# Crossbar DMAs in place of TensorE transposes for q, k and the attention output of the last five half batches of a fused attention and feed-forward kernel

## Chip, cores and metric

One core of one Trainium2 chip. The metric is device time in microseconds (us), median of several runs; lower is better. Most runs of one kernel lie within 1% of each other. Ratios are the mean time of one kernel's runs over the mean of the other's in the same rounds, so they are not quite the ratio of the medians that are quoted beside them.

In the profile PE is TensorE (PEld its weight loads), DVE VectorE, ACT ScalarE, POOL GpSimd, and SPq the queue from which SyncE issues DMAs. L709 is line 709 of the kernel's file. PSUM is the memory that PE writes its results to. A DMA lands when its data has arrived. A crossbar transpose is a DMA that transposes on the way (`dma_start_transpose`). The two kernels have different line numbers for the same statement, so each line below is told in words too.

## The reference

Sliding-window attention with four sink positions, then a gated feed-forward layer on all tokens. Batch 4, 8 heads, 768 tokens, head size 64, model width 512, hidden width 2048.

```python
scores = scale * np.matmul(q, k.transpose(0, 1, 3, 2))
keep = is_sink | in_window                       # 4 sinks, window of 128
a = softmax(np.where(keep, scores, -1e9))
attn = np.matmul(a, v)
x = attn.transpose(0, 2, 1, 3).reshape(B * S, H * D)
h = x @ w_in
return (h * (1 / (1 + np.exp(-beta * h)))) @ w_out
```

Inputs and output are float32; the kernel computes its matmuls in bfloat16.

## The kernel before

The work is cut into 8 half batches of 384 tokens, and each half batch into 4 pairs of heads (32 units `u`). For a unit: transpose q and k (`T`), scores (`SC`, `SS`), weighted values (`AV`), transpose the output (`OT`). When four units are done, a half batch can go through the feed-forward layer (`HQ`, then `OQ`). The kernel does not run in the order of the source: while it is built, a planner (`Graph`) records all operations with an estimated time each, lists them per engine in the order of a simulated run, and emits that order. On the chip each engine executes its own list in order, whatever is ready.

The q and k of a unit go through PE into a PSUM bank and are copied out by DVE or ACT; the output goes the same way:

```python
def T(u):                                       # 6 transposes and one copy of 128x768
    hb, hp = u // 4, u % 4
    bs = take(1)                                # a PSUM bank
    mp = P[:, bs[0], :].bitcast(BF16)
    for i, n in enumerate("qk"):
        for c in range(NK):
            add("pe", lambda e, i=i, n=n, c=c: nc.tensor.transpose(
                mp[:, i * HALF + c * 128:i * HALF + (c + 1) * 128],
                x16[n][hb % NX][:, c, 2 * hp:2 * hp + 2, :].rearrange("p h d -> p (h d)"), ident[:, :]),
                mm_ns(128), r=[(n + "16", hb % NX, hp, c), "ident"], x=[("B", bs[0])])
    any_of(copies(qkT[u % NT]..., mp[:, 0:2 * HALF]..., {"dve": 868, "act": 690}),
           w=[("qkT", u % NT)], x=[("B", bs[0])])
    # ... (cut)

def OT(u):                                      # 3 transposes and one copy of 128x384
    # ... (cut)
    for m in range(NK):
        add("pe", lambda e, m=m: nc.tensor.transpose(
            mp[:, m * 128:(m + 1) * 128], onorm[on][:, m, :, :].rearrange("p h d -> p (h d)"), ident[:, :]),
            mm_ns(128), r=[("on", on), "ident"], x=[("B", bs[0])])
    any_of(copies(xT[:, hp, t0:t0 + HALF], mp[:, 0:HALF], {"dve": 407, "act": 370}),
           w=[("xT", hp, 2 * b + half)], x=[("B", bs[0])])
```

All DMAs are issued from SyncE. The planner charges each of them 550 ns of that queue, and its bytes to one shared stream:

```python
def place(self, o, at):
    o.at = at
    if o.dma:
        self.free[o.eng] = at + (1150 if o.eng == "gp" else 550)
        self.dma_free = max(self.dma_free, at + 1100) + 1.15 * o.ns
        o.end = self.dma_free + 1000
    else:
        o.end = self.free[o.eng] = at + o.ns
```

The softmax here doesn't subtract the row's maximum and nothing guards it: scores larger than these inputs give would overflow.

## Time and profile before

240.95 us median (240.21 to 241.29, 4 runs); the profiled run had a span of 239.3 us.

| what | before |
|---|---|
| PE busy | 228.4 us, 95% of the span |
| PE busy from 50 to 230 us | 10.00 of every 10 us, save one stretch each of 9.96 and 9.74 |
| DVE / ACT / POOL busy | 62% / 68% / 33% |
| DMA engines | full until about 101 us, then 2 to 15% in most stretches |
| transposes on PE | 288 (192 of q and k, 96 of the output) |

The first view is the table of stretches: from and to in us, its length, then for PE, PEld, DVE, ACT and POOL the busy us with the number of instructions in brackets, the clock granted to PE, the share of the DMA engines, GB/s.

```profile
40.00:50.00 10.00, 8.80 (x51) 4.52 (x50) 8.57 (x18) 6.61 (x12) 0.66 (x1) 1.00 1.08 332
...
90.00:100.00 10.00, 10.00 (x94) 6.06 (x92) 7.44 (x16) 8.42 (x17) 1.87 (x5) 1.00 1.12 267
...
120.00:130.00 10.00, 10.00 (x113) 6.33 (x110) 6.47 (x14) 7.40 (x15) 3.58 (x9) 1.00 0.07 26
```

In the first 50 us PE still waits; from 50 us on it never stops. What PE does less of there should come off the time one for one, and what DVE and ACT do less of should not.

The cost of a transpose on this full PE is not the duration that the groups list. Groups (line, engine, operation, output and inputs, shapes, count, busy us, mean ns; then idle time before it) and the timeline of PE (start, us, what, count):

```profile
L690 PE MATMUL P<-ident,onorm 128*128 128x128 bf16 x96 | 10.7, 220 | 2.3 <-DVE onorm L677 2.2
```

```profile
113.88 0.34 PE L548 MATMUL P<-ident,q_0 128*128 128x128 bf16 x3
114.06 0.33 PE L548 MATMUL P<-ident,k_0 128*128 128x128 bf16 x3
114.22 1.03 PE L729 MATMUL P<-w_out,g 128*128 128x512 bf16 x4
```

One transpose is listed with 220 ns, but three q and three k transposes start at 113.88 and the next work starts at 114.22: 0.34 us for six, 57 ns each. They overlap in the engine. In the chain of waits 24 of them in a row account for 1.34 us, 56 ns each.

### The profile page before, as it was taken

Reading aid. Unit: us, or ns where it says so; the run is one execution under the profiler, and the core shown is the slowest. Engines: PE = TensorE matmul, PEld = TensorE weight load, DVE = VectorE, ACT = ScalarE, POOL = GpSimd, SP = SyncE. Lnnn points to the kernel's source line nnn. Section 1 sums busy time; section 2 is a strip of 40 time slices with the busy share of each in tenths; the row PEclk is TensorE's granted clock in tenths of the full one; section 3 lists DMA queues with packets and bytes.
Section 4 is the critical chain, followed back from the end, with each engine's and each line's share of the span. In section 5 each row is a group of like instructions: output and inputs, shape, how many; then the busy total and the mean of one; then the engine's idle time right before and its main releaser. Section 6 shows DMA issues by size and latency. Waiting matters only on the chain.

```text
span 239.3 us, 4895 instructions
## 1 busy us (share of the span) xinstructions
PE 228.4 (95%) x1936; PEld 132.3 (55%) x1936; DVE 149.4 (62%) x305; ACT 163.7 (68%) x293; POOL 79.6 (33%) x172
## 2 busy tenths in 40 slices
PE   7977898999999999999999999999999999999994
PEld 5554554556565666565566555565555555555541
DVE  3895598886896987898667585464433633443320
ACT  3858977679788888997768686856544644554431
POOL 6575933032875593263643043530000000000000
PEclk9999999999999999999999999999999999999999
DMA  6999999999999999801011010110111011011112
GB/s 169 255 341 230 313 394 386 337 218 337 240 286 249 315 313 285 180 4 45 4 44 45 2 44 3 44 47 0 47 44 44 18 42 40 36 44 47 44 44 88
DMA packets 49558, 33.87 MB, mean 142 GB/s; under 512 B 25968, under 2 KB 42368, under 8 KB 49536
## 3 DMA queue, kind: packets, MB, share of 16 engines
q1 hardware_dynamic: 49536, 33.57, 48.6%
q8 instruction: 15, 0.25, 0.5%
q14 instruction: 7, 0.06, 0.1%
HBM read 27.27 MB, written 6.29 MB: 140 GB/s over the span
## 4 chain that ended last, share of the span: by engine, by line
PE 80%; SPq 9%; DVE 4%; DMA 3%; ACT 2%; issue 1%
PE P L729 34%; PE P L709 31%; SPq L491 7%; PE P L600 4%; PE P L548 4%; PE P L671 3%; DMA g<-in_moe_w_in_dram 3%; PE P L690 2%; SPq L501 2%; DVE g L716 1%; PE P L632 1%; PE P L661 1%; ACT t L714 1%; ACT E L609 1%; DVE w_in L438 1%
## 5 line engine op out<-in xcount | busy, mean ns | idle before, releaser
L716 DVE SCALAR_TENSOR_TENSOR g<-t,P 128x384 bf16<-128x384 f32 x128 | 69.9, 552 | 59.2 <-ACT t L714 56.6
L714 ACT ACTIVATE t<-P,hbeta 128x384 f32<-128x384 f32 x128 | 74.0, 587 | 44.5 <-PE P L709 41.1
L709 PE MATMUL P<-xT,w_in 128*128 128x384 bf16 x512 | 98.5, 326 | 1.1 <-DVE w_in L438 1.0
L729 PE MATMUL P<-w_out,g 128*128 128x512 bf16 x384 | 97.3, 379 | 0.0
L615 POOL TENSOR_SCALAR_AFFINE_SELECT E<-E 128x512 bf16<-128x512 bf16 (+1 forms) x112 | 54.5, 516 | 56.1 <-ACT E L609 55.3
L709 PEld LDWEIGHTS P<-xT,w_in 128*128 128x128 bf16 x512 | 48.0, 98 | 37.5 <-DVE w_in L438 1.8
L729 PEld LDWEIGHTS P<-w_out,g 128*128 128x128 bf16 x384 | 36.5, 98 | 33.3 <-DVE g L716 0.5
L609 ACT ACTIVATE E<-P 128x768 bf16<-128x768 f32 x64 | 45.7, 769 | 3.1 <-PE P L600 2.8
L438 DVE COPY qkT<-P 128x768 bf16<-128x768 bf16 x19 | 18.0, 951 | 4.0 <-PE P L548 4.0
L671 PE MATMUL P<-vaug,E 128*128 128x65 bf16 x352 | 18.8, 193 | 0.8 <-DVE vaug L438 0.7
L433 ACT ACTIVATE osb<-P 128x512 f32<-128x512 f32 x21 | 12.5, 597 | 10.2 <-PE P L729 10.1
L671 PEld LDWEIGHTS P<-vaug,E 128*128 128x128 bf16 x352 | 16.7, 97 | 3.4 <-DVE vaug L438 0.9
L677 DVE TENSOR_TENSOR onorm<-P,rden 128x384 bf16<-128x384 f32 x32 | 17.8, 557 | 1.0
L600 PE MATMUL P<-qkT 64*128 64x128 bf16 (+1 forms) x256 | 16.3, 239 | 1.0 <-ACT E L609 0.9
L433 ACT ACTIVATE xT<-P 128x384 bf16<-128x384 bf16 x20 | 9.9, 495 | 6.7 <-PE P L690 6.7
L600 PEld LDWEIGHTS P<-qkT 64*128 64x128 bf16 x256 | 8.6, 94 | 10.6 <-issue 5.1
L433 ACT ACTIVATE qkT<-P 128x768 bf16<-128x768 bf16 x13 | 10.2, 814 | 5.2 <-PE P L548 5.1
L635 ACT ACTIVATE ES<-P 128x128 bf16<-128x128 f32 (+1 forms) x32 | 12.1, 407 | 2.2 <-PE P L632 2.1
L690 PE MATMUL P<-ident,onorm 128*128 128x128 bf16 x96 | 10.7, 220 | 2.3 <-DVE onorm L677 2.2
L661 PE MATMUL P<-vS,ES 128*128 128x130 bf16 x64 | 12.7, 220 | 0.0
L690 PEld LDWEIGHTS P<-ident,onorm 128*128 128x128 bf16 x96 | 7.0, 98 | 7.7 <-DVE onorm L677 4.2
L885 PE MATMUL P<-ones 128*128 128x256 bf16 x47 | 8.8, 323 | 1.1 <-POOL ones L444 1.1
(60 smaller groups left out, 148.3 us busy)
## 6 DMA issues: line engine op xcount, KB each, us to landing
v_stage<-in_v_dram SPq DMA_DIRECT2D x24, 256.0 KB, 6.7
out_dram<-osb SPq DMA_DIRECT2D x24, 256.0 KB, 2.0
q_stage<-in_q_dram SPq DMA_DIRECT2D x7, 768.0 KB, 6.8
k_stage<-in_k_dram SPq DMA_DIRECT2D x7, 768.0 KB, 8.6
wst<-in_moe_w_in_dram SPq DMA_DIRECT2D x5, 512.0 KB, 8.9
wst<-in_moe_w_out_dram SPq DMA_DIRECT2D x4, 512.0 KB, 6.8
g<-in_moe_w_out_dram SPq DMA_DIRECT2D x4, 512.0 KB, 6.9
g<-in_moe_w_in_dram SPq DMA_DIRECT2D x3, 512.0 KB, 8.2
```

The source lines that it names most:

```text
L433: return lambda e: e.activation(dst, src, AF.Copy, bias=0.0, scale=scale)
L438: return lambda e: e.tensor_copy(dst, src)
L600: add("pe", lambda e, dst=dst, kt=kt, kc=kc, rows=rows, q0=q0, nq=nq: e.matmul(dst, kt[rows, 1, kc:kc + 128], qkT[u % NT][rows, 0, q0:q0 + ...
L609: add("act", lambda e, src=src, dst_=dst_: e.activation(dst_, src, AF.Exp, bias=0.0, scale=SCALE), act_ns(256 * n), w=[(k_, z, j) for k_ i ...
L615: add("gp", lambda e, d=d, sg=sg, at_=at_: e.affine_select(d, d, [[0, 2 * len(at_)], [sg, 128]], ALU.is_ge, 0.0, base=min(sg, 0), channel_ ...
L671: e.matmul(A[:, c0:c0 + D + 1], E[z][:, i, hh, :], vaug[vz][:, kb % NK, 2 * hp + hh, :], start=a, stop=o, skip_group_check=True), 39,
L677: add("dve", lambda e: e.tensor_tensor(onorm[on][:, :, :, :].rearrange("p m h d -> p (m h) d"), av[:, :, 0:D], rden[on][:, :].unsqueeze(2) ...
L690: add("pe", lambda e, m=m: nc.tensor.transpose(mp[:, m * 128:(m + 1) * 128], onorm[on][:, m, :, :].rearrange("p h d -> p (h d)"), ident[:, ...
L709: add("pe", lambda e, c=c: e.matmul(hp, w_in16[:, c, m * 128:(m + 1) * 128], xT[:, c, t0:t0 + HALF], start=(c == 0), stop=(c == 3)), mm_ns ...
L714: add("act", lambda e: e.activation(tt[ti][:, :], hp, AF.Tanh, bias=0.0, scale=hbeta[:, m:m + 1]), act_ns(HALF) + 93, r=["hbeta"], w=[("t" ...
L716: add("dve", lambda e: e.scalar_tensor_tensor(gt[T_ % NG][:, m, :], tt[ti][:, :], 1.0, hp, ALU.add, ALU.mult), dve_ns(HALF), r=[("t", ti)] ...
L729: add("pe", lambda e, m=m: e.matmul(P[:, bk, :], gt[T_ % NG][:, m, t * 128:(t + 1) * 128], w_out16[:, m, :], start=(m == 0), stop=(m == NM ...
```

## The change

Its intent: take 180 of the 288 transposes off PE, with the copies out of PSUM that belong to them, and let the DMA engines, idle after 101 us, do them. The first three half batches stay on PE, since the DMA engines are full then. The core of the diff (cut):

```diff
-            self.free[o.eng] = at + (1150 if o.eng == "gp" else 550)
+            self.free[o.eng] = at + o.hold
 ...
+    CUT = 3
 ...
+    def XP(hb, n, c):
+        z0, i = 4 * hb % NT, "qk".index(n)
+        src = x16[n][hb % NX][:, c, :, :].rearrange("p h d -> p (h d)")      # 128 x 512
+        dst = qkT[:, z0:z0 + 4, i, c * 128:(c + 1) * 128]
+        add("sp", lambda e: e.dma_start_transpose(dst, src), 950,
+            r=[...], w=[...], dma=f"x{n}{hb % 3}{c}", hold=1310)
 ...
     def OT(u):
+        if u >= 4 * CUT:
+            dst = xT[:, hp, t0:t0 + HALF].rearrange("p (m t) -> p m t", m=NK)
+            src = onorm[on][:, :, :, :].rearrange("p m h d -> p (m h d)")     # 128 x 384
+            add("sp", lambda e: e.dma_start_transpose(dst, src), 750, r=[("on", on)],
+                w=[...], dma=f"xo{on}", hold=1310)
+            return
```

So the new DMAs are 30 of 128x512 (four 128x128 tiles; one third of q or k of a half batch) and 20 of 128x384 (three tiles; the output of one unit). The planner charges each 1.31 us of the SyncE queue (`hold`) and 1.15 x 950 or 750 ns of the DMA stream. Three things come along: q and k of the last five half batches are loaded in blocks of 128 tokens, 256 KB each with runs of 256 bytes, instead of 768 KB with runs of 768 bytes; there are 12 instead of 8 slots for transposed q and k and 5 instead of 3 for outputs; and the transposed outputs are kept for 5 half batches instead of all 8, to pay for that.

More of the change, by code (lines that the diff above doesn't have):

```diff
@@ L24 @@
     __slots__ = ("eng", "fn", "deps", "signal", "count", "waits", "sem", "vc", "dma", "seq", "end", "ns", "alts",
-                 "group", "tail", "preds", "ready", "left", "succ", "at")
+                 "group", "tail", "hold", "preds", "ready", "left", "succ", "at")
 class Graph:
@@ L52, in begin, with add @@
         self.group += 1
-    def add(self, eng, fn, ns=0, r=(), w=(), x=(), dma=None, alts=None):
+    def add(self, eng, fn, ns=0, r=(), w=(), x=(), dma=None, alts=None, after=(), hold=550):
         o = Op()
@@ L60, in add @@
         o.eng, o.fn, o.dma, o.ns, o.alts = eng, fn, dma, ns, alts or {eng: (fn, ns)}
-        o.signal, o.count, o.waits, o.vc = False, 0, [], None
+        o.signal, o.count, o.waits, o.vc, o.hold = False, 0, [], None, hold
         o.group = self.group if eng == "pe" else None
@@ L71, in add @@
             deps += [(p, False) for p in self.writers.get(k, ())]
+        for k in after:
+            deps += [(p, False) for p in self.readers.get(k, []) + self.writers.get(k, [])]
         for k in x:
@@ L346, in _program @@
     NU = 2 * NPAIR
-    NSTG, NX, NV, NT, NE, NON, NG, NTT, NOS, NKS, NWS = 2, 2, 3, 8, 4, 3, 3, 3, 4, 4, 6
+    NSTG, NX, NV, NT, NE, NON, NG, NTT, NOS, NKS, NWS = 2, 2, 3, 12, 4, 5, 3, 3, 4, 4, 6
+    NXT = 5
+    CUT = 3
     FAST = 1
@@ L357, in _program @@
     headm = sb("headm", (128, 2), BF16)
-    xT = sb("xT", (128, 4, NTOK), BF16)
+    xT = sb("xT", (128, 4, NXT * HALF), BF16)
     w_in16 = sb("w_in16", (128, 4, DF), BF16)
     w_out16 = sb("w_out16", (128, NM, NOUT), BF16)
-    stg = {n: sb(n + "_stage", (128, H, NK, D), F32, NSTG) for n in "qk"}
-    stg["v"] = sb("v_stage", (128, NK, H, D), F32, NSTG)
+    stg = {n: sb(n + "_stage", (128, NK, H, D), F32, NSTG) for n in "qkv"}
+    stg_p = {n: [t[:, :, :, :].rearrange("p a b d -> p (a b d)").rearrange("p (h j d) -> p h j d", j=NK, d=D)
+                 for t in stg[n]] for n in "qk"}
     x16 = {n: sb(n + "16_", (128, NK, H, D), BF16, NX) for n in "qk"}
     vaug = sb("vaug", (128, NK, H, D + 1), BF16, NV)
-    qkT = sb("qkT", (128, 2, HALF), BF16, NT)
+    qkT = sb("qkT", (128, NT, 2, HALF), BF16)
     E = sb("E", (128, 6, 2, 128), BF16, NE)
@@ L380, in _program, with add @@
     P = ps("P", (128, 8, 512))
-    def add(eng, fn, ns, r=(), w=(), x=(), dma=None):
-        return G.add(eng, fn, ns, r, w, x, dma)
+    def add(eng, fn, ns, r=(), w=(), x=(), dma=None, after=(), hold=550):
+        return G.add(eng, fn, ns, r, w, x, dma, None, after, hold)
     def any_of(alts, r=(), w=(), x=()):
@@ L482, in load @@
         b, t0, z = hb // 2, hb % 2 * HALF, hb % NSTG
-        if n == "v":
-            src = v[b, :, t0 + i * 128:t0 + (i + 1) * 128, :].rearrange("h p d -> p h d")
-            dst, keys, ns = stg[n][z][:, i, :, :], [i], 262144 / 240
+        if n == "v" or hb >= CUT:
+            src = {"q": q, "k": k, "v": v}[n][b, :, t0 + i * 128:t0 + (i + 1) * 128, :].rearrange("h p d -> p h d")
+            dst, keys, ns = stg[n][z][:, i, :, :], [("stb", n, z, i)], 262144 / 240
         else:
@@ L488, in load @@
             src = {"q": q, "k": k}[n][b, hs, t0:t0 + HALF, :].rearrange("h (p j) d -> p h (j d)", j=NK)
-            dst = stg[n][z][:, hs, :, :].rearrange("p h j d -> p h (j d)")
+            dst = stg_p[n][z][:, hs, :, :].rearrange("p h j d -> p h (j d)")
             keys, ns = ([i], 196608 / 350) if i is not None else (range(4), 786432 / 350)
-        add("sp", lambda e: e.dma_start(dst, src), ns,
-            w=[("stg", n, z, j) for j in keys], dma=f"d{n}{z}{'' if i is None else i}")
+            keys = [("stg", n, z, j) for j in keys]
+        after = [("stg", n, z, j) for j in range(4)] if hb in range(CUT, CUT + NSTG) and n != "v" else ()
+        add("sp", lambda e: e.dma_start(dst, src), ns, w=keys, dma=f"d{n}{z}{'' if i is None else i}", after=after)
     def load_w(j):
@@ L516, in cast @@
             src, dst = stg[n][z][:, i, :, :], vaug[hb % NV][:, i, :, 0:D]
-            r, w = [("stg", n, z, i), ("vones", hb % NV)], [("v", hb % NV, i)]
+            r, w = [("stb", n, z, i), ("vones", hb % NV)], [("v", hb % NV, i)]
         elif hb == 0:
             hs = slice(2 * i, 2 * i + 2)
-            src = stg[n][z][:, hs, :, :].rearrange("p h j d -> p j h d")
+            src = stg_p[n][z][:, hs, :, :].rearrange("p h j d -> p j h d")
             dst = x16[n][hb % NX][:, :, hs, :]
@@ L523, in cast @@
         else:
-            src, dst = stg[n][z][:, :, i, :], x16[n][hb % NX][:, i, :, :]
-            r, w = [("stg", n, z, j) for j in range(4)], [(n + "16", hb % NX, j, i) for j in range(4)]
-        if hb == 0 and n != "v":
-            ns = {"act": 413, "dve": 400}
-        else:
-            ns = {"act": 540, "dve": 340, "gp": 612}
+            dst, w = x16[n][hb % NX][:, i, :, :], [(n + "16", hb % NX, j, i) for j in range(4)]
+            if hb >= CUT:
+                src, r = stg[n][z][:, i, :, :], [("stb", n, z, i)]
+            else:
+                src, r = stg_p[n][z][:, :, i, :], [("stg", n, z, j) for j in range(4)]
+        ns = {"act": 413, "dve": 400} if hb == 0 and n != "v" else {"act": 540, "dve": 340, "gp": 612}
         any_of(copies(dst, src, ns), r=r, w=w)
@@ L537, in cast, with qk_keys, first_keys @@
                     r=[("vS", z), ("v", hb % NV, 0)], w=[("vSd", z, hh)])
+    def qk_keys(u, name="qkT", every=NT):
+        return [(name, u % every, a, c) for a in range(2) for c in range(NK)]
+    def first_keys(u):
+        ks = u % NKS
+        kd = kS[ks][:, :].rearrange("p (a w) -> p a w", w=32)[:, 0:2, 0:NSINK]
+        add("gp", lambda e: e.tensor_tensor(
+            kd, qkT[:, u % NT, 1:2, 0:NSINK].to_broadcast([128, 2, NSINK]),
+            headm[:, :].unsqueeze(2).to_broadcast([128, 2, NSINK]), ALU.mult), 200,
+            r=[("kS", ks), ("qkT", u % NT, 1, 0), "headm0", "headm"], w=[("kSd", ks)])
+    def XP(hb, n, c):
[3 more added lines that the diff above has]
+        add("sp", lambda e: e.dma_start_transpose(dst, src), 950,
+            r=[(n + "16", hb % NX, j, c) for j in range(4)], w=[("qkT", z0 + j, i, c) for j in range(4)],
+            dma=f"x{n}{hb % 3}{c}", hold=1310)
+        for j in range(4):
+            mark(("qkTu", 4 * hb + j, i, c), ("qkT", z0 + j, i, c))
+        if hb % 2 == 0 and (n, c) == ("k", 0):
+            for j in range(4):
+                first_keys(4 * hb + j)
     def T(u):
@@ L551, in T @@
                     mm_ns(128), r=[(n + "16", hb % NX, hp, c), "ident"], x=[("B", bs[0])])
-        any_of(copies(qkT[u % NT][:, :, :].rearrange("p a (s j) -> p a s j", j=NK),
+        any_of(copies(qkT[:, u % NT, :, :].rearrange("p a (s j) -> p a s j", j=NK),
                       mp[:, 0:2 * HALF].rearrange("p (a j s) -> p a s j", a=2, j=NK), {"dve": 868, "act": 690}),
-               w=[("qkT", u % NT)], x=[("B", bs[0])])
+               w=qk_keys(u), x=[("B", bs[0])])
+        for key in qk_keys(u):
+            mark(("qkTu", u) + key[2:], key)
         if hb % 2 == 0:
-            ks = u % NKS
-            kd = kS[ks][:, :].rearrange("p (a w) -> p a w", w=32)[:, 0:2, 0:NSINK]
-            add("gp", lambda e: e.tensor_tensor(
-                kd, qkT[u % NT][:, 1:2, 0:NSINK].to_broadcast([128, 2, NSINK]),
-                headm[:, :].unsqueeze(2).to_broadcast([128, 2, NSINK]), ALU.mult), 200,
-                r=[("kS", ks), ("qkT", u % NT), "headm0", "headm"], w=[("kSd", ks)])
+            first_keys(u)
         give(bs)
@@ L591, in SC @@
                 own = u if kb >= NK * half else u - 4
-                kt = qkT[own % NT]
+                kt = qkT[:, own % NT, 1, :]
                 kc = (kb % NK) * 128
@@ L600, in SC @@
                     add("pe", lambda e, dst=dst, kt=kt, kc=kc, rows=rows, q0=q0, nq=nq: e.matmul(
-                        dst, kt[rows, 1, kc:kc + 128],
-                        qkT[u % NT][rows, 0, q0:q0 + 128 * nq].rearrange("p (s w) -> p s w", w=128),
+                        dst, kt[rows, kc:kc + 128],
+                        qkT[rows, u % NT, 0, q0:q0 + 128 * nq].rearrange("p (s w) -> p s w", w=128),
                         start=True, stop=True), mm_ns(128 * nq) / 2 + 24,
-                        r=[("qkT", u % NT), ("qkT", own % NT)], x=[("B", bs[2 * j + hh])])
+                        r=qk_keys(u) + (qk_keys(own) if own != u else []), x=[("B", bs[2 * j + hh])])
         for j, grp in enumerate(GROUPS[half]):
@@ L631, in SS @@
         bs = take(1)
-        add("pe", lambda e: e.matmul(P[:, bs[0], q0:HALF], kS[ks][:, :], qkT[u % NT][:, 0, q0:HALF], start=True,
+        add("pe", lambda e: e.matmul(P[:, bs[0], q0:HALF], kS[ks][:, :], qkT[:, u % NT, 0, q0:HALF], start=True,
                                      stop=True), mm_ns(HALF - q0),
-            r=[("kSd", ks), ("qkT", u % NT)], x=[("B", bs[0])])
+            r=[("kSd", ks)] + qk_keys(u), x=[("B", bs[0])])
         add("act", lambda e: e.activation(ES[z][:, q0:HALF], P[:, bs[0], q0:HALF], AF.Exp, bias=0.0, scale=SCALE),
@@ L686, in OT @@
         on = u % NON
+        t0 = (2 * b + half) % NXT * HALF
+        if u >= 4 * CUT:
+            dst = xT[:, hp, t0:t0 + HALF].rearrange("p (m t) -> p m t", m=NK)
+            src = onorm[on][:, :, :, :].rearrange("p m h d -> p (m h d)")
+            add("sp", lambda e: e.dma_start_transpose(dst, src), 750, r=[("on", on)],
+                w=[("xT", hp, (2 * b + half) % NXT)], dma=f"xo{on}", hold=1310)
+            return
         bs = take(1)
@@ L692, in OT @@
                 mm_ns(128), r=[("on", on), "ident"], x=[("B", bs[0])])
-        t0 = b * S + half * HALF
         any_of(copies(xT[:, hp, t0:t0 + HALF], mp[:, 0:HALF], {"dve": 407, "act": 370}),
-               w=[("xT", hp, 2 * b + half)], x=[("B", bs[0])])
+               w=[("xT", hp, (2 * b + half) % NXT)], x=[("B", bs[0])])
         give(bs)
@@ L705, in HQ @@
         bs = take(1)
-        t0 = T_ * HALF
+        t0 = T_ % NXT * HALF
         hp = P[:, bs[0], 0:HALF]
@@ L711, in HQ @@
                 start=(c == 0), stop=(c == 3)), mm_ns(HALF),
-                r=[("w16", m // 4, c // 2), ("xT", c, T_)], x=[("B", bs[0])])
+                r=[("w16", m // 4, c // 2), ("xT", c, T_ % NXT)], x=[("B", bs[0])])
         spare_ = [("wst", NWS // 2 + z) for z in range(NWS // 2)] if (T_, m) == (NG - 1, 0) else []
@@ L746, in xl @@
         if hb:
+            if hb >= CUT:
+                return [(hb, n, c) for n in "qkv" for c in range(NK)]
             return [(hb, "q", None), (hb, "k", None)] + [(hb, "v", c) for c in range(NK)]
@@ L753, in _program @@
     OS = [(T_, t, j) for T_ in range(NSB) for t in range(3) for j in range(4)]
-    n_cast, n_w = [0], [0]
+    XPS = [(hb, n, c) for hb in range(CUT, NSB) for n in "qk" for c in range(NK)]
+    n_cast, n_w, n_x = [0], [0], [0]
     BACKLOG, AHEAD, MARGIN = 6000, 300, 200
@@ L760, in head @@
         if s == "T":
-            if i >= NU or i - NT + 4 >= min(done["SC"], done["SS"]):
+            if i >= 4 * CUT or i - NT + 4 >= min(done["SC"], done["SS"]):
                 return None
@@ L766, in head @@
             tb = banks_at(1)
-            fn = lambda: (T(i), mark(("qkTu", i), ("qkT", i % NT)))
+            fn = lambda: T(i)
         elif s in ("SC", "SS"):
@@ L770, in head @@
                 return None
-            t, tb = G.at([("qkTu", i)]), banks_at(4 if s == "SC" else 1)
+            t, tb = G.at(qk_keys(i, "qkTu", NU) + ([("kSd", i % NKS)] if s == "SS" else [])), banks_at(4 if s == "SC" else 1)
             fn = lambda: (SC if s == "SC" else SS)(i)
@@ L781, in head @@
             t, tb = G.at([("onu", i)]), banks_at(1)
-            fn = lambda: OT(i)
+            if t and i >= 4 * CUT:
+                t, tb = 0, 0
+            if i // 4 >= NXT and done["H"] < NM * (i // 4 - NXT + 1):
+                return None
+            fn = lambda: (OT(i), mark(("xTu", i % 4, i // 4), ("xT", i % 4, i // 4 % NXT)))
         elif s == "H":
@@ L788, in head @@
                 return None
-            t = G.at([("xT", c, T_) for c in range(4)] + [("w16", m // 4, 0), ("w16", m // 4, 1)])
+            t = G.at([("xTu", c, T_) for c in range(4)] + [("w16", m // 4, 0), ("w16", m // 4, 1)])
             tb = banks_at(1)
@@ L825, in background @@
                     load(*x)
-                    mark(("in",) + x, ("stg", x[1], x[0] % NSTG, x[2] or 0))
+                    mark(("in",) + x, ("stb" if x[1] == "v" or x[0] >= CUT else "stg", x[1], x[0] % NSTG, x[2] or 0))
                     done["load"] += 1
@@ L831, in background @@
                 hb, n, c = CASTS[i]
-                t = G.at([("in", hb, n, None if n != "v" and hb else c)])
+                t = G.at([("in", hb, n, None if n != "v" and 0 < hb < CUT else c)])
                 ok = done["T"] >= 4 * (hb - NX + 1) if n != "v" else done["AV"] >= 4 * (hb - NV + 2)
@@ L837, in background @@
                     moved = True
+            if n_x[0] < len(XPS):
+                hb, n, c = XPS[n_x[0]]
+                if n_cast[0] > CASTS.index(XPS[n_x[0]]) and min(done["SC"], done["SS"]) >= 4 * (hb - NT // 4 + 2):
+                    XP(hb, n, c)
+                    n_x[0] += 1
+                    moved = True
+                    if n_x[0] % 6 == 0:
+                        done["T"] += 4
             if n_w[0] < 16:
@@ L847, in _program @@
         load(*x)
-        mark(("in",) + x, ("stg", x[1], 0, x[2]))
+        mark(("in",) + x, ("stb" if x[1] == "v" else "stg", x[1], 0, x[2]))
         if n_ == 1:
@@ L854, in _program @@
     done["load"] = 11
-    def T_(u):
-        T(u)
-        mark(("qkTu", u), ("qkT", u % NT))
     for u in range(2):
@@ L863, in _program @@
         cast(0, "k", u)
-    T_(0)
-    T_(1)
+    T(0)
+    T(1)
     beta_in()
@@ L871, in _program @@
         SS(u)
-        T_(u + 2)
+        T(u + 2)
     SC(2)
@@ L884, in _program @@
     OT(3)
+    for c in range(4):
+        mark(("xTu", c, 0), ("xT", c, 0))
     G.fill(lambda e: e.matmul(P[:, 7, 0:256].rearrange("p (a b) -> p a b", a=2), ones[:, :],
```

## The prediction

> **What bounds the kernel now.** TensorE (PE). In the table of stretches PE is busy 10.00 of 10 us in nearly every stretch from 50 to 230 us, at a granted clock of 1.00; only the first 50 us (7.5 to 9.8 of 10) have idle time. The chain of waits agrees: 80% PE. DVE (62%), ACT (68%) and POOL (33%) are off the path after 50 us. The DMA engines are full until about 101 us and nearly idle afterwards.
>
> **What the change removes.** For half batches 3 to 7 (20 of 32 head pairs) it removes 6 q/k transposes and 3 output transposes each: 180 of 288 on PE. A matmul's listed time (220 ns) includes pipeline latency; the cost on a full PE is the spacing. In the chain 24 of them take 1.34 us, 56 ns each; in the timeline six take 0.34 to 0.35 us. So 180 x 56 ns = 10.1 us, all after about 60 us, where PE is the limit. Also gone are 20 PSUM evictions of qkT (0.95 us on DVE, 0.81 on ACT) and 20 of xT (0.35 or 0.50): about 27 us off DVE and ACT, which gives slack, no time.
>
> **What it adds.** 30 crossbar transposes of 128x512 and 20 of 128x384 bf16, 5.9 MB, on the SyncE queue; the planner charges each 1.31 us of queue and about 1 us of DMA: 65 us of a queue that today mostly waits for output evictions (133 us). q and k of those half batches are loaded in 256 KB blocks of 256-byte runs, like v, instead of 768 KB of 768-byte runs. Where only v was in flight (94 to 100 us) the DMA moved 225 to 256 GB/s; with q and k 330 to 370. So a half batch's loads cost an estimated 9.6 us instead of 7.5. With transposes (10 us) and output that is 20 to 23 us of DMA per half batch: the DMA stays busy until about 170 us, but the PE has some 24 us of work per half batch, and its order holds feed-forward matmuls between a transpose and its reader.
>
> **Critical path.** All 10.1 us come out, less about 1 us of new stalls (the PE order is fixed). The first 50 us stay. Prediction: 240.98 - 10.1 + 1 = 231.9 us; range 229.5 to 237. Faster by over 2%: 0.81; within 2%: 0.14; slower: 0.05.
>
> **What would show it.** PE busy near 218; 108 transposes left; PE still 10.00 of 10 from 50 us on; DMA share high to 165-175 us; q/k transposes issued in about 1.3 us each, landed 4 to 6 us later; DVE and ACT together 27 us less busy; no PE wait above 1 us on qkT or xT.
>
> **What would make it wrong.** The cost of a crossbar transpose; no trace here shows one. The Trainium skill, "VectorE: DVE Perf Modes", section "The three transpose paths", gives 1309 ns for one 128x128; 180 tiles one after the other at that price (estimate from that page) would need 236 us. The skill's "DMA: Bandwidth & Descriptors", section "Latency and other measured facts", gives 261 GB/s; then 5.9 MB need 23 us (estimate from that page). I take the planner's middle value. If transposes take 1.5 times as long, or hold up loads behind them, lateness adds up over five half batches and PE waits at the scores (readers of qkT) between 70 and 180 us: 233 to 242 us. Another risk: output stores blocking the in-order queue.

## The result

232.51 us median (231.59 to 234.15, 4 runs) against 240.95; ratio 0.9661, 95% interval 0.9602 to 0.972. Repeated on the set of runs of e5 below: 232.44 us (231.33 to 232.95, 6 runs), ratio 0.9629, interval 0.9596 to 0.9663. The prediction was 231.9 us, in a range of 229.5 to 237.

| what | before | after |
|---|---|---|
| time, median | 240.95 us | 232.51 us |
| span of the profiled run | 239.3 us | 230.6 us |
| PE busy | 228.4 us | 216.6 us |
| DVE / ACT / POOL busy | 149.4 / 163.7 / 79.6 us | 135.0 / 156.6 / 73.3 us |
| transposes on PE | 288 | 108 |
| DMA packets | 49,558 | 94,997 |

PE's records lack 26 of the 384 matmuls of the second feed-forward matrix (1730 records beside 1756 weight loads). Each lost record leaves a hole of about 0.05 us, which is why the stretches read 9.95 and not 10.00 even where nothing waits. The table of stretches after:

```profile
40.00:50.00 10.00, 8.86 (x49) 4.44 (x50) 8.56 (x17) 6.66 (x11) 0.66 (x1) 1.00 1.08 333
...
90.00:100.00 10.00, 9.56 (x72) 5.15 (x70) 6.67 (x16) 6.67 (x15) 1.36 (x2) 1.00 0.83 198
...
120.00:130.00 10.00, 9.09 (x55) 4.71 (x55) 5.10 (x12) 7.04 (x15) 0.66 (x1) 1.00 1.14 238
```

The start is the same. Two stretches lose time to waits, 90 to 100 and 120 to 130; the DMA engines, which before were at 7 or 8% from 110 to 170 us, now stay busy until about 180 us.

The issues of the transposes and how long they hold the queue, from the answers for the tiles of transposed q and k and of the outputs (duration in ns, minimum, median and maximum; then from issue to landing):

```profile
L564 SPq DMA_TRANSPOSE qkT<-q x15: 1258/1267/2106, 58.7 to 164.6; - x15
L564 SPq DMA_TRANSPOSE qkT<-k x15: 1264/1267/2151, 62.2 to 165.9; - x15
...
DMA to landing us min/median/max: 2.5/2.6/4.5
```

```profile
L721 SPq DMA_TRANSPOSE xT<-onorm x20: 1179/1253/1907, 91.6 to 189.6; - x20
...
DMA to landing us min/median/max: 2.3/2.7/4.7
```

The planner's 1.31 us of queue was right (1.27 us and a gap of some 0.05 us). It lands after 2.6 us, and PE does not wait for a transpose's landing: the list of PE's waits has no DMA in it. What it does have is this:

```profile
PE P L727 <- DVE onorm L707: 2.0, 3, 1.0
PE P L765 <- DVE g L752: 1.3, 2, 0.9
PE P L581 <- DVE k L444: 1.1, 2, 0.8
PE P L935 <- POOL ones L450: 1.1, 1, 1.1
```

(Columns: who waited, for whom, us in total, times, longest.) The first and the last two waits lie in the first 50 us; from 50 to 80 us PE waits for nothing. The second is new: two waits, 1.3 us together, of the second feed-forward matmul for `g`, the activation that DVE writes. The longer of the two is at 124.5 us. DVE's timeline there:

```profile
118.47 2.50 DVE L752 SCALAR_TENSOR_TENSOR g<-t,P 128x384 bf16<-128x384 f32 x4 [0.96 <-ACT t L750]
123.27 0.43 DVE L444 CAST vaug<-v_stage 128x512 bf16<-128x512 f32 x1 [2.29 <-DMA v_stage<-in_v_dram]
124.45 0.43 DVE L444 CAST vaug<-v_stage 128x512 bf16<-128x512 f32 x1 [0.74 <-DMA v_stage<-in_v_dram]
124.79 1.94 DVE L752 SCALAR_TENSOR_TENSOR g<-t,P 128x384 bf16<-128x384 f32 x4
```

and the SyncE queue before that:

```profile
112.95 6.26 SPq L721 DMA_TRANSPOSE xT<-onorm  x4
119.25 0.58 SPq L774 DMA_DIRECT2D out_dram<-osb  x1
119.87 2.13 SPq L499 DMA_DIRECT2D v_stage<-in_v_dram  x3
```

Four transposes of outputs and a store stand in the queue right before the loads of v (six transposes of q and k stand before those), and held it until 119.8 us. The loads landed after DVE had reached the casts that need them. DVE executes in order, so it stood 2.29 and 0.74 us before these casts, with the `g` that PE needed behind them. This is how the transposes cost PE time: not by landing late themselves, but by holding up a plain load behind them. The other wait (0.39 us at 97.2 us) has no DMA in it: the next matmul in PE's list needed an activation whose ACT and DVE steps had only just begun.

The sum comes out close: 180 x 56 ns = 10.1 us off PE, less the two new waits of 0.86 and 0.39 us, is 8.8 us; the spans differ by 8.7 us. That it agrees to 0.1 us is partly luck. PE's busy time fell by 11.8 us and its idle time grew by 3.1 us; with an estimated 1.3 us moved from idle to busy for the lost records, these are 10.5 us gained and 1.8 us lost.

### The profile page after: what moved, and what is told of

Read it like the earlier page. It is cut to its first block, busy times and chain, and to the rows that moved or that the text cites. A ratio compares the mean times of both kernels' runs of the same rounds, so it can differ in the third digit from the quotient of the medians.

```text
span 230.6 us, 4557 instructions
## 1 busy us (share of the span) xinstructions
PE 216.6 (94%) x1730; PEld 122.0 (53%) x1756; DVE 135.0 (59%) x285; ACT 156.6 (68%) x282; POOL 73.3 (32%) x163
## 2 busy tenths in 40 slices
DMA packets 94997, 39.76 MB, mean 172 GB/s; under 512 B 81648, under 2 KB 87808, under 8 KB 94976
## 4 chain that ended last, share of the span: by engine, by line
PE 76%; DMA 10%; ACT 4%; SPq 4%; DVE 2%; issue 1%; POOL 1%
PE P L765 34%; PE P L745 30%; DMA wst<-in_moe_w_in_dram 4%; PE P L630 4%; DMA k_stage<-in_k_dram 4%; SPq L499 4%; PE P L701 4%; DMA v_stage<-in_v_dram 2%; DVE g L752 1%; ACT t L750 1%; PE P L691 1%; ACT qkT L439 1%; ACT E L639 1%; PE P L662 1%; PE P L581 1%
## 5 line engine op out<-in xcount | busy, mean ns | idle before, releaser
L745 PE MATMUL P<-xT,w_in 128*128 128x384 bf16 x512 | 96.3, 326 | 0.9 <-DVE w_in L444 0.3
L765 PE MATMUL P<-w_out,g 128*128 128x512 bf16 x358 | 91.8, 379 | 2.7 <-DVE g L752 1.3
L645 POOL TENSOR_SCALAR_AFFINE_SELECT E<-E 128x512 bf16<-128x512 bf16 (+1 forms) x112 | 55.2, 522 | 66.7 <-ACT E L639 66.1
L765 PEld LDWEIGHTS P<-w_out,g 128*128 128x128 bf16 x384 | 35.6, 98 | 37.1 <-DVE g L752 2.8
L444 DVE CAST q<-q_stage 128x512 bf16<-128x512 f32 (+1 forms) x17 | 9.0, 540 | 7.0 <-DMA q_stage<-in_q_dram 7.0
L444 DVE CAST vaug<-v_stage 128x512 bf16<-128x512 f32 x16 | 7.3, 456 | 8.2 <-DMA v_stage<-in_v_dram 8.1
L665 ACT ACTIVATE ES<-P 128x128 bf16<-128x128 f32 (+1 forms) x32 | 10.9, 410 | 0.4 <-PE P L662 0.4
L441 POOL TENSOR_SCALAR_AFFINE_SELECT vaug<-v_stage 128x512 bf16<-128x512 f32 x3 | 2.1, 693 | 25.5 <-DMA v_stage<-in_v_dram 25.5
L651 DVE TENSOR_TENSOR E<-E,maskS 128x512 bf16<-128x512 bf16 x15 | 7.0, 463 | 5.0 <-ACT E L639 4.8
L444 DVE CAST k<-k_stage 128x512 bf16<-128x512 f32 (+1 forms) x14 | 6.5, 464 | 5.7 <-DMA k_stage<-in_k_dram 5.5
```

Of the source, the lines that this page charges most:

```text
L444: return lambda e: e.tensor_copy(dst, src)
L645: add("gp", lambda e, d=d, sg=sg, at_=at_: e.affine_select(d, d, [[0, 2 * len(at_)], [sg, 128]], ALU.is_ge, 0.0, base=min(sg, 0), channel_ ...
L745: add("pe", lambda e, c=c: e.matmul(hp, w_in16[:, c, m * 128:(m + 1) * 128], xT[:, c, t0:t0 + HALF], start=(c == 0), stop=(c == 3)), mm_ns ...
L765: add("pe", lambda e, m=m: e.matmul(P[:, bk, :], gt[T_ % NG][:, m, t * 128:(t + 1) * 128], w_out16[:, m, :], start=(m == 0), stop=(m == NM ...
```

## The experiments

Theory A: the gain is the PE time of the 180 transposes, 56 ns each, less the new waits. Rival B: it is the relief of DVE and ACT, and of the PSUM banks, by the copies that are gone. Rival C: it is the deeper buffers, or another plan. After these, what limits the new path was looked at. All kernels that ran gave the reference's result.

### e1, e2, e3: the parts of the change alone

One more constant lets q and k on one side and the outputs on the other be put back on PE; with `NSB` (8) no half batch goes by crossbar.

```diff
-    CUT = 3
+    CUT, OCUT = NSB, NSB      # e1: neither;  e2: 3, NSB (q and k only);  e3: NSB, 3 (output only)
 ...
-        if u >= 4 * CUT:                  # in OT
+        if u >= 4 * OCUT:
 ...
-            if t and i >= 4 * CUT:        # in the planner's head of OT
+            if t and i >= 4 * OCUT:
```

> The changed kernel with its new buffer counts and tile layouts (12 instead of 8 qkT slots, 5 onorm buffers, xT for 5 half batches), but with no crossbar transpose: all 288 transposes on PE and the old loads. Theory A (the gain is the PE time of 180 transposes): all of it is gone, 240 to 242 us, ratio 0.997 to 1.005. Rival C (the gain is the deeper buffers or the new plan): the gain stays at least in part, below 237 us.

> Crossbar for q and k alone; the attention outputs go back to PE (60 transposes and 20 evictions back). Theory A: 60 x 56 ns = 3.4 us of the gain lost, so about 232.5 + 3.4 = 235.9 us (234.5 to 237). If the output transposes were worth nothing: 232.5. If the q/k path through the DMA queue were what limits: it would be equal or faster, since the queue loses 20 x 1.3 us.

> Crossbar for the attention output alone; q and k on PE with the old loads. Theory A: only 3.4 us gained, 241.0 - 3.4 = 237.6 us (236.5 to 238.8). If the gain came from the q/k side's DMA layout or evictions alone: about 241.

| run | PE transposes gone | time, median | ratio to before (95%) |
|---|---|---|---|
| e1, neither | 0 | 240.50 us | 0.9973 (0.9939 to 1.0007) |
| e2, q and k | 120 | 235.05 us | 0.9751 (0.9723 to 0.978) |
| e3, output | 60 | 238.02 us | 0.9868 (0.9841 to 0.9895) |
| the change | 180 | 232.51 us | 0.9661 (0.9602 to 0.972) |

All three fell where theory A put them. Rival C falls: with all of the new buffers and no crossbar transposes, e1 cannot be told from before. With the ratio and the median of before in that set (241.31 us), e2 gains 6.0 us and e3 3.2 us, which is 50 and 53 ns per transpose. Their traces say the same: PE was busy 6.1 and 3.2 us less than before (222.3 and 225.2 us), and the list of PE's waits has none for `g` above 0.3 us. The parts add up to 9.2 us; the change gave 8.2 us by its first ratio and 9.0 by its second.

### e4: the PE time put back, the copies left out

The same 180 transposes are also done on PE, into a bank that nobody reads. Two rules of the planner change with it (not in the cut below): a cast into a slot of q or k waits until the added transposes have read the slot, and the output's transposes are no longer planned ahead of their input.

```diff
+    def DT(u):                            # as T, without the copy; its result is not used
+        ...
+        for i, n in enumerate("qk"):
+            for c in range(NK):
+                add("pe", ... nc.tensor.transpose(mp[...], x16[n][hb % NX][...], ident[:, :]), ...)
+        give(bs)
 ...
                 w=[...], dma=f"xo{on}", hold=1310)
+            bs = take(1)
+            for m in range(NK):
+                add("pe", ... nc.tensor.transpose(mp[...], onorm[on][...], ident[:, :]), ...)
+            give(bs)
             return
```

> The changed kernel, and the same 180 transposes also done on PE into a PSUM bank that nobody reads (no eviction comes back, the crossbar result is what is used). Theory A: the PE time comes back, 232.5 + 10.1 = 242.6 us (240.5 to 243.5). Rival B (the gain is the 40 evictions off DVE and ACT and the banks that they held): it stays near 233.

Measured: 246.31 us (245.63 to 248.49), ratio 1.0229 (1.0187 to 1.0271). This speaks against rival B: the copies are still gone, and the kernel is slower than before. But the size missed, 246.3 against a range of 240.5 to 243.5. PE busy came back as it should (228.9 us, against 228.4 before). PE's idle time is 15.2 us, against 10.9 before, and most of the difference is in one place:

```profile
120.00:130.00 10.00, 7.72 (x58) 4.08 (x58) 3.90 (x8) 8.45 (x17) 4.11 (x8) 1.00 0.83 156
130.00:140.00 10.00, 8.43 (x99) 5.92 (x99) 6.86 (x17) 5.21 (x9) 3.23 (x10) 1.00 0.71 154
```

with two waits in the list of PE's waits that are not in the changed kernel's,

```profile
PE P L739 <- DVE onorm L720: 1.8, 1, 1.8
PE P L785 <- DVE g L772: 1.7, 1, 1.7
```

and the chain of waits there (start, us, what) goes through the queue and through in-order lists again:

```profile
115.18 4.66 DMA v_stage<-in_v_dram
...
121.00 0.57 DVE g L772
121.56 0.66 SPq L734
...
123.52 5.95 DMA q_stage<-in_q_dram
...
129.49 0.87 DVE q L444
130.35 0.46 DVE g L772
```

The first wait, for `g` at 121.6 us, ends behind a load of v that landed at 119.8 us and its cast on ACT. The second ends at 131.6 us: transposes of outputs (L734 in that kernel) hold the queue, the load of q behind them comes late, DVE stands before the cast of q, and what PE waits for stands behind that cast. It is the kind of chain that the changed kernel has, but what PE waits for the second time is `onorm`, which the added transposes read. So part of the extra waiting comes from the experiment itself, and perhaps from the two changed rules; no run separates them. e4 shows that the gain goes when PE's work comes back, not its size.

The added transposes also take their PSUM banks back. That the banks' relief did not make the gain is seen in the trace of before: PE stood idle for 0.3 us in all from 50 to 230 us, so no wait for a bank was there to be removed.

### e5: the changed kernel again

The reference of the next three runs.

> The changed kernel again, unedited, as the reference of this set of runs: 232.5 us (231.5 to 233.5), ratio near 0.965.

232.44 us, as told above. The wait of PE for `g` was there again: twice, 1.4 us together, the longest 1.0.

### e6: copies put back, PE left alone

Each cast of q, k and v of the last five half batches is done again, whole on DVE and half on ACT, into buffers that nobody reads.

```diff
         any_of(copies(dst, src, ns), r=r, w=w)
+        if hb >= CUT:
+            f1, n1 = copies(dump1[:, :, :], src, {"dve": 430})["dve"]
+            add("dve", f1, n1, r=r + ["dump1"], w=["dump1"])
+            f2, n2 = copies(dump2[:, :, :], src[:, 0:4, :], {"act": 400})["act"]
+            add("act", f2, n2, r=r + ["dump2"], w=["dump2"])
```

> The changed kernel with extra copies and nothing more on PE: each cast of q, k and v of the last five half batches is done again into a buffer that nobody reads, 45 full ones on DVE and 45 half ones on ACT, an estimated 33 us (more than the 27 us of evictions that the change took away). Theory A (only PE time counts; DVE and ACT had room): 232.5 to 234.5 us. Rival B (relief of DVE and ACT made the gain): 237 to 241.

Measured: 233.11 us (232.4 to 235.6), ratio 0.9674 (0.9629 to 0.9719), beside 0.9629 of e5. The extra copies took 0.42 us each at the median and 39.9 us in all, which is more than the change removed; the planner moved other casts between the engines in return (DVE 133.9 to 152.4 us, ACT 156.6 to 165.8, POOL 73.7 to 76.7). DVE and ACT together were then busy 318.2 us, more than the 313.1 of the kernel before. The time moved by 0.7 us, inside the intervals. With e1 to e4 and the full PE of before this settles it: PE time is what the change gained.

### e7: the same DMAs, planned without their queue time

```diff
-        add("sp", lambda e: e.dma_start_transpose(dst, src), 950, ... hold=1310)      # XP
+        add("sp", lambda e: e.dma_start_transpose(dst, src), 375, ... hold=550)
-            add("sp", lambda e: e.dma_start_transpose(dst, src), 750, ... hold=1310)  # OT
+            add("sp", lambda e: e.dma_start_transpose(dst, src), 281, ... hold=550)
```

> The changed kernel, but its planner is told that a transpose costs what an ordinary load costs (0.55 us of queue, and bytes at 350 GB/s) in place of the 1.31 us and 1.09 us; the same instructions in another order. If the order needs the measured queue time: the queue runs late by about 0.75 us per transpose, PE waits, 235 to 240 us. If the slack between a transpose and its reader is ample whatever the order: within 1 us of the changed kernel.

Measured: 259.08 us (258.47 to 262.06), ratio 1.0752 (1.0702 to 1.0802): slower than before by 7.5%, and far outside the 235 to 240 that was expected. The direction was right, the size much too small. The DMAs and matmuls are the same, and so is the price of a transpose (median 1.27 us of queue). What differs is the order, and with it which engine does a few of the copies. Both charges of a transpose were lowered at once, the queue time and the bytes, so the run does not tell the two apart. The worst place, first DVE, then PE:

```profile
138.25 0.43 DVE L444 CAST vaug<-v_stage 128x512 bf16<-128x512 f32 x1 [6.59 <-DMA v_stage<-in_v_dram]
```

```profile
133.53 0.82 PE L745 MATMUL P<-xT,w_in 128*128 128x384 bf16 x4
139.81 5.25 PE L745 MATMUL P<-xT,w_in 128*128 128x384 bf16 x16 [5.46 <-DVE g L752]
```

DVE stands 6.59 us before a cast of v, PE 5.46 us behind it. And there is a second cost, which the expectation had left out: the 16 matmuls after the wait take 5.25 us, where the same 16 take 2.76 us elsewhere. The table of stretches shows the granted clock:

```profile
136.00:138.00 2.00, 0.00 (x0) 0.00 (x0) 0.00 (x0) 0.00 (x0) 0.29 (x1) 1.00 0.93 212
140.00:144.00 4.00, 4.00 (x14) 1.87 (x13) 2.71 (x7) 1.23 (x3) 0.00 (x0) 0.50 1.31 246
```

The Trainium skill, "TensorE: Matmul & The Clock Gate", section "Why this matters for your kernels", asks for no PE-idle gaps over about 3 us, since after one the clock falls to half. This trace agrees here: the gap of 5.46 us began at 134.35 us, and the granted clock was 0.50 from 138.1 to 144.8 us. But shorter gaps were enough elsewhere. In the same trace the clock was also 0.50 from 90.3 to 93.7, from 110.8 to 120.9 and from 162.0 to 165.3 us, and the longest waits of PE just before these were 2.2, 2.2 and 2.9 us. In e10 below it was 0.50 from 81.3 to 88.0 us, though no single wait of PE was above 0.8 us from 42 to 88 us. Over the whole run PE was busy 225.9 us for work that took 216.4 us in e5, so an estimated 9.5 us of the loss is slow clock and the rest waiting. The four slow stretches hold 18.0 us of PE's busy time; half of that is 9.0 us, which agrees.

### e8 and e11: loads assumed to land 2 us later

If the in-order wait on a late load is what is left, an order in which casts stand later should remove it.

```diff
         new, planned = [], set()          # in arrange(), which makes the final order
+        self.lat = 3000
 ...
-            o.end = self.dma_free + 1000
+            o.end = self.dma_free + getattr(self, "lat", 1000)
```

> The changed kernel, ordered as if every DMA landed 2 us later than the planner thought, so that a cast stands later in its engine's queue, behind work that is ready. In the changed kernel's trace PE stood still for 0.86 us at 124.5 us and 0.39 us at 97.2 us, both times for a feed-forward eviction on DVE; at 124.5 us DVE itself waited for a v load behind the transposes in the SyncE queue. If that in-order wait is what was left of the 10.1 us: 231.0 to 231.7 us, and no PE wait for such an eviction above 0.3 us. If not: 232.5 or more.

> The run that lands later, unedited, beside the other two and on another set of runs of before: 231.6 us (230.8 to 232.3), ratio 0.960.

Measured: 231.58 us (230.56 to 232.05), ratio 0.9602 (0.9569 to 0.9635), beside e5's 0.9629 (0.9596 to 0.9663); and again, in another set, 232.03 us (231.59 to 233.83), ratio 0.9629 (0.9592 to 0.9666). The wait at 124.5 us is gone in both traces. The other one stayed: PE waits for `g` once, 0.4 us, at 96.9 us in e8 and 100.2 us in e11, so that part of the expectation (no such wait above 0.3 us) was missed. In e8 DVE reached the casts of v with waits of 0.48 and 0.79 us where it had 2.29 and 0.74:

```profile
120.75 0.43 DVE L445 CAST vaug<-v_stage 128x512 bf16<-128x512 f32 x1 [0.48 <-DMA v_stage<-in_v_dram]
121.97 0.43 DVE L445 CAST vaug<-v_stage 128x512 bf16<-128x512 f32 x1 [0.79 <-DMA v_stage<-in_v_dram]
```

So the cause of the wait is shown. PE's idle time from 50 us to the end was 6.7 us in the changed kernel and 6.8 in e5, and 5.8 in e8 and in e11. That its removal makes the kernel faster is not shown: the first set says 0.9 us by the medians, the second is level with the changed kernel's ratio, and the intervals overlap. In e11's trace PE waited 1.4 us once for a weight cast (L746 for DVE w_in) and 1.4 us once for a cast of k; both belong to the first 50 us, where such waits vary from run to run by as much as the wait that was removed. No version was found that is clearly faster than the change.

### e9: one DMA for a whole half batch of q or k

The layouts of the cast and of the transposed q and k are turned so that 12 tiles stand in one row, and three DMAs become one. Three other numbers were changed with it, so the time alone would not single out the size: the two charges of the planner, and e8's later landing.

```diff
-    x16 = {n: sb(n + "16_", (128, NK, H, D), BF16, NX) for n in "qk"}
+    x16 = {n: sb(n + "16_", (128, H // 2, NK, 2, D), BF16, NX) for n in "qk"}
-    qkT = sb("qkT", (128, NT, 2, HALF), BF16)
+    qkT = sb("qkT", (128, 2, NT, HALF), BF16)
 ...
-    def XP(hb, n, c):
+    def XP(hb, n):
+        src = x16[n][hb % NX][:, :, :, :, :].rearrange("p a c h d -> p (a c h d)")     # 128 x 1536
+        dst = qkT[:, i, z0:z0 + 4, :].rearrange("p u (c t) -> p (u c) t", t=128)
+        add("sp", lambda e: e.dma_start_transpose(dst, src), 1695, ... hold=2600)
```

> q and k of a half batch each transposed by one DMA of 128x1536 (12 tiles of 128x128) in place of three of 128x512 (4 tiles); ordered as in the run that lands later, with a planner's charge of 2.6 us of queue. In the changed kernel a transpose of 4 tiles held the queue 1.26 us and one of 3 tiles 1.25 us, while its packets took an estimated 0.65 us of the 16 engines. Theory F (the queue time is a fixed price per DMA): about 1.3 us each, 10 of them, the queue gets 26 us back, and the time is 231 to 232.5 us. Theory T (price per tile, 0.31 us): 3.8 us each, no queue time gained, and the order is late by 1.2 us for each: 232 to 236 us. In both the PE work is the same, so no gain over 1 us is expected.

Measured: 231.77 us (231.06 to 232.11), ratio 0.96 (0.9565 to 0.9635): not to be told from the changed kernel or from e8, as expected. Two transposes of 12 tiles, one behind the other, in the queue, and all 10 (duration in ns, minimum, median and maximum):

```profile
102.45 1.29 SPq L565 DMA_TRANSPOSE qkT<-k  x1
103.79 2.01 SPq L565 DMA_TRANSPOSE qkT<-q  x1
```

```profile
L565 SPq DMA_TRANSPOSE qkT<-q x5: 1443/2166/2792, 62.7 to 142.1; - x5
L565 SPq DMA_TRANSPOSE qkT<-k x5: 1288/1460/3012, 65.1 to 140.5; - x5
```

The shortest of the 10 took 1.29 us, against 1.26 for four tiles and 1.18 for three; theory T had asked for 3.8 us each. But that is the least of ten: four took 1.29 to 1.46 us and six took 2.0 to 3.0 us. The DMA engines were busy beside all six (share 1.05 to 1.44), but that alone does not explain it: in the changed kernel two transposes of four tiles took 1.27 us beside a share of 1.29 and 1.43. All 10 held the queue 21.2 us, where the 30 small ones held it 42.7 us in the changed kernel. So theory T is out. Theory F is nearer, but its fixed 1.3 us for each of the ten, 13 us in all, is not what was measured: 2.1 us each. PE was full either way, so it bought no time here.

### e10: one half batch more

```diff
-    CUT = 3
+    CUT = 2
```

> One more half batch (the third) by crossbar: 36 more PE transposes gone. PE time alone: 36 x 56 ns = 2.0 us less, 230.4 us. Rival (the DMA engines are full until about 58 us with weights and inputs, and this half batch's transposes come in the same queue ahead of the next loads, which are then late): no gain, 236 to 243 us, with PE waiting between 70 and 90 us.

Measured: 244.61 us (242.98 to 245.01), ratio 1.0123 (1.0078 to 1.0169). It has 36 fewer transposes on PE than the changed kernel and is 12 us slower. Now PE also waits for the DMAs themselves, where the transposes are read:

```profile
PE P L662 <- DMA qkT<-k: 2.7, 1, 2.7
...
PE P L745 <- DMA xT<-onorm: 1.1, 2, 0.8
```

```profile
80.00:90.00 10.00, 8.29 (x38) 3.52 (x38) 2.36 (x6) 6.47 (x13) 5.06 (x10) 0.66 0.78 145
```

PE was busy 8.23 us in the stretch from 70 to 80 us, 8.29 from 80 to 90 (at a granted clock of 0.66), and 7.20 from 150 to 160. The two waits for DMAs are 3.8 of the 12 us. The clock was 0.50 from 81.3 to 88.0 and from 152.9 to 156.3 us, with 8.3 us of PE's work in it, an estimated 4 us; the rest is waits behind ACT, DVE and POOL. The third half batch's loads are issued right behind the weights, up to 48.9 us, its transposes until 57.9, and the fourth's loads only start at 61.7 us (50.5 in the changed kernel). With this planner six half batches were worse than five; whether a better order exists for six was not tried, nor whether the queue or the full DMA engines set the limit.

## Why the prediction was right

- **The bound.** PE from 50 us on; right. e6 put 39.9 us of copies on DVE and ACT without a visible cost.
- **The gain.** 180 x 56 ns = 10.1 us; right. e2 and e3 measured 50 and 53 ns per transpose with all waits in it, e4 took the gain back. The step that mattered was to read a transpose's cost from the spacing of starts on a full engine. The listed 220 ns would have promised 40 us. The Trainium skill, "TensorE: Matmul & The Clock Gate", section "Part 4: PE-mode transpose", gives 390 ns in isolation and about 275 ns in one kernel; as prices on a full PE both are far above what this case shows.
- **New stalls, about 1 us.** The two that were found measure 1.25 us, so the size held, but it was a guess, and not from where it was looked for. The prediction watched for PE waiting at the readers of transposed q and k; PE waited for `g`, because a load of v stood behind transposes in the queue and its cast stood before `g` on DVE.
- **The queue.** 1.3 us per transpose; right (1.27). In all 69.4 us, predicted 65.
- **Landing.** Predicted 4 to 6 us, measured 2.6. The prediction let each wait behind loads; an estimated 0.65 us of the engines per transpose, issued 1.3 us apart, probably left them room; no run tests this.
- **DMA until 165 to 175 us.** It was about 180 us (share 0.72 from 170 to 180, 0.22 after).
- **DVE and ACT 27 us less.** The copies themselves fell by 26.7 us (42.3 to 15.6, from the groups), but DVE and ACT together by 21.5 us (14.4 and 7.1): the planner gave them casts that POOL had done, and POOL fell by 6.3 us. The term was right, the sum forgot that the planner reassigns.
- **The fear.** That a transpose of 128x128 costs 1309 ns each, from the Trainium skill's "VectorE: DVE Perf Modes", section "The three transpose paths": it does not add up so. A DMA of 3 or 4 tiles holds the queue 1.25 or 1.27 us at the median, and one of 12 tiles 2.1 us. The other fear, that a late queue would cost 233 to 242 us, was too mild: e7's order lost 26 us against the changed kernel, an estimated third of it to the clock.

## What to carry to other kernels

On an engine that is full, price an operation by the spacing of its starts, not by its listed duration. When work moves to an in-order DMA queue, look less at whether its own results come in time than at what stands behind it in the queue, and at which engine will stand still, in order, before the operation that needs it. And if a static order is made from a cost table, what each new kind of DMA takes, of the queue above all, must be measured and put in first: the same DMAs and matmuls gave 232 us with it and 259 us with the price of an ordinary load.

## What the Trainium skill lacked or had wrong

- "DMA: Bandwidth & Descriptors", section "Issuing engines are not separate DMA queues", says that the sequencer's time to issue a DMA is usually small beside the DMA. For a crossbar transpose it is the larger part: 1.27 us of queue for 128x512, while from 62 to 67 us, with nothing else in flight, four of them kept the 16 engines busy for 0.52 of the time, 0.65 us each. No page gives a queue time of a transpose that was measured on this chip (the only cycles of issuing one, on that page, compare a later chip with "previous generations"), nor how little it grows with the tiles: 1.18, 1.26 and 1.29 us at the least and 1.25, 1.27 and 2.1 us at the median for 3, 4 and 12.
- "Advanced Engine Details and Errata", section "X-Bar Transpose (TRN2)", calls transposes as fast as ordinary DMAs and expects 350 to 400 GB/s. In that stretch they moved 105 GB/s at a share of 0.52, an estimated 202 GB/s at a share of 1. In e9 two transposes of 384 KB, one behind the other, moved 208 GB/s at a share of 1.14 (103.8 to 107.5 us). Back to back from one queue 105 GB/s is what these runs got at 128 KB each.
- "VectorE: DVE Perf Modes", section "The three transpose paths": the page gives 1309 ns for a 128x128 by DMA and does not say whether that is time in the queue or until the data has landed, nor how it grows with more tiles. No run here has a DMA of one tile; those of 3 and 4 tiles held the queue 1.25 and 1.27 us at the median and landed some 2.6 us after issue, so the figure must not be multiplied by the tiles.
- "TensorE: Matmul & The Clock Gate", section "Part 4: PE-mode transpose": this part prices a transpose at 390 and 275 ns and does not say what it adds among other matmuls on a full PE; here 56 ns by the spacing of starts, and 50 and 53 ns by the times of e2 and e3.
